# Linear attention and two MLPs on one core: decays loaded once, weights landing where their halves go, a third attention buffer, and an opening in another order

## The chip, the cores and the metric

The kernel runs on one core of one Trainium2 chip. The core has five engines with their own instruction streams: TensorE (PE, matmuls; PEld are its weight loads), VectorE (DVE), ScalarE (ACT), GpSimd (POOL) and SyncE (SP, which here issues nearly all DMAs). The metric is the device time of one execution in microseconds (us), as the median of several runs. A profile is one further execution with the hardware profiler on.

## The reference

```python
# q, k, v, alpha: (4 batches, 8 heads, 768 tokens, 48), alpha between 0.8 and 1.0
for t in range(S):
    state = alpha[:, :, t, :, None] * state + einsum('bhd,bhe->bhde', k[:, :, t], v[:, :, t])
    y[:, :, t] = einsum('bhd,bhde->bhe', q[:, :, t], state)
x = y as 3072 tokens x 384
h = x @ w_in            # 384 x 2048
x = (h * sigmoid(1.702 * h)) @ w_out
h = x @ w2_in           # the same sizes, other weights
out = (h - tanh(h)) @ w2_out
```

All is fp32. The weights reach the kernel as 64-bit floats.

## The kernel before, in words

The attention is cut into 24 chunks g of 128 tokens, six to a batch. The 8 heads lie in 4 pairs. For a chunk, DVE forms running products of the decay along the tokens with two scans, one forwards (`a_scan(g, 1)`) and one backwards (`a_scan(g, 0)`, whose row is loaded reversed as a second copy of the same decays), a reciprocal between them, and multiplies keys and queries by them (`a_scale`, L249 and L250; on POOL from chunk 8 on). These steps are called `prep(g, 0..3)`. Then PE forms the scores (L279, or L298 from chunk 8 on), which are masked (POOL L285, or DVE L301 from chunk 8 on), the masked scores times the values (L332), the carried state times the queries (L325), and the new part of the state (L341). ACT takes the result out of the bank (`a_evac`, L360), SP writes it to `xt` in device memory (L365) and reads it back turned (`a_back`, L378) as the MLP's input, of which ACT forms a high half (`xhi`, L382) and DVE the low rest (`xlo`, L383). From chunk 8 on DVE also turns the keys by 32x32 transposes (L308), because the whole chunk is then done in one go.

Each MLP layer goes over six tiles j of 512 tokens and 16 columns of blocks m: a step s is one pair (j, m), 96 steps to a layer. A step has nine 128x512 matmuls of gemm1 (L392: high x high, high x low, low x high over three blocks), the activation on ACT (L406 for layer 1), its split into `ghi` (ACT L409) and `glo` (DVE L410), and nine matmuls of gemm2 (L399), which PE does three steps later (LAG 3).

The weights of a layer arrive as 768 KB per m (L156) in one of three `raw` buffers. DVE rebuilds fp32 from the 64-bit form (`w_bits`, L163 and L164; `w_join`, L176), ACT copies the high half `whi` (L193) and DVE subtracts for `wlo` (L194). For layer 1 this happens during tile j=0, one m per step, in `conv(1)`; until then only three are ready. A raw buffer comes free when `w_join` of its m is done, and SP, which takes its orders strictly in turn, waits there.

Opening (chunks 0 to 3) and tile j=0 (with chunks 4 to 7 and the start of 8 and 9 beside it) are kept in the order of the program text by `in_order(begin)`. What comes after is ordered by a scheduler from the program text and its own priorities. From chunk 8 on every chunk's scans, transposes and masks run on DVE beside the MLP steps of layer 1 while PE takes the chunk's matmuls between its gemms. Attention chunk data lie in two late buffers of the `arena` (chunk 2 in `gt` and `xs`), and the load of chunk g+2 is issued when chunk g is done.

## Time and profile before

| | us |
|---|---|
| median of three runs | 952.52 |
| the three runs | 954.36, 948.78, 952.52 |
| the profiled execution | 957.78 |
| its span from first to last instruction | 956.1 |
| PE, DVE, ACT busy in it | 913.8 (96%), 676.5 (71%), 449.5 (47%) |
| DMA moved | 101.91 MB |

The profiled execution lies 5.3 us above the median. A row of a timeline gives start, duration, engine, line, operation, tiles, and in brackets the idle time of that engine before it and what ended it. Rows of PE that follow each other without a bracket ran without a gap. PEclk is the share of TensorE's full clock that was granted.

### The profile page before, as it was taken

The numbers are of one execution on the slowest core, as the hardware profiler recorded it, in microseconds if no ns is written. First come the engines' busy times: TensorE is split into PE (matmuls) and PEld (weight loads), VectorE is DVE, ScalarE is ACT, GpSimd is POOL, SyncE is SP. The second block draws the span as 40 slices with busy tenths as digits, with TensorE's granted clock in tenths as the row PEclk, the third lists the DMA queues.
The fourth block names the chain that finished last, engine by engine and source line by source line (L and its number), as shares of the span: only waits on it lengthen the run. The fifth ranks groups of instructions, "written<-read, shape, count | busy, mean of one in ns | idle before, by whom it ended". The sixth has DMA issues, their size and how long they took to land.

```text
span 956.1 us, 13257 instructions
## 1 busy us (share of the span) xinstructions
PE 913.8 (96%) x4870; PEld 728.1 (76%) x4870; DVE 676.5 (71%) x1124; ACT 449.5 (47%) x906; POOL 85.9 (9%) x70
## 2 busy tenths in 40 slices
PE   5569999999989999999999999999999999999997
PEld 4347777777768777777888888888888888888885
DVE  7799997844774787484159986766776777766663
ACT  4445533323434434343344564554566566544542
POOL 1201211101120111110100200100100001000000
PEclk9999999989989999999999999999999999999999
DMA  9767434422643565434125410200322420000001
GB/s 268 236 201 240 137 87 125 120 68 79 200 132 141 159 196 198 128 113 158 32 93 181 138 60 1 78 22 1 113 96 89 166 99 1 33 1 1 34 1 37
DMA packets 58107, 101.91 MB, mean 107 GB/s; under 512 B 5024, under 2 KB 37408, under 8 KB 58032
## 3 DMA queue, kind: packets, MB, share of 16 engines
q1 hardware_dynamic: 58032, 100.97, 33.7%
q8 instruction: 40, 0.66, 0.3%
q14 instruction: 35, 0.29, 0.1%
HBM read 86.79 MB, written 14.16 MB: 106 GB/s over the span
## 4 chain that ended last, share of the span: by engine, by line
PE 61%; DVE 0%; issue 0%; ACT 0%; ACTq 0%
PE bank L399 30%; PE bank L392 29%; PE bank L332 1%; PE bank L298 0%; PE bank L325 0%; PE bank L341 0%; DVE xs L442 0%; DVE arena L301 0%; PE bank L268 0%; ACT xs L445 0%; ACTq L671 0%
## 5 line engine op out<-in xcount | busy, mean ns | idle before, releaser
L410 DVE TENSOR_TENSOR glo<-gt,ghi 128x512 fp32r<-128x512 f32 x192 | 140.1, 732 | 151.0 <-ACT ghi L409 146.8
L392 PE MATMUL bank<-xhi,whi 128*128 128x512 f32 x576 | 229.2, 398 | 9.5 <-ACT xhi L382 8.8
L399 PE MATMUL bank<-ghi,whi 128*128 128x512 f32 x576 | 233.1, 405 | 0.0
L399 PE MATMUL bank<-ghi,wlo 128*128 128x512 f32 x576 | 229.0, 397 | 0.0
L392 PE MATMUL bank<-xlo,whi 128*128 128x512 f32 x576 | 228.5, 397 | 0.4 <-DVE xlo L383 0.4
L399 PE MATMUL bank<-glo,whi 128*128 128x512 f32 x576 | 228.5, 397 | 0.0
L392 PE MATMUL bank<-xhi,wlo 128*128 128x512 f32 x576 | 228.1, 396 | 0.0
L409 ACT CAST ghi<-gt 128x512 fp32r<-128x512 f32 x192 | 119.2, 621 | 220.8 <-DVE gt L421 133.1
L392 PEld LDWEIGHTS bank<-xhi,whi 128*128 128x128 f32 x576 | 109.2, 190 | 35.6 <-ACT xhi L382 9.0
L399 PEld LDWEIGHTS bank<-ghi,whi 128*128 128x128 f32 x576 | 109.2, 190 | 28.4 <-issue 1.9
L392 PEld LDWEIGHTS bank<-xlo,whi 128*128 128x128 f32 x576 | 109.3, 190 | 26.4 <-DVE xlo L383 1.2
L399 PEld LDWEIGHTS bank<-glo,whi 128*128 128x128 f32 x576 | 109.4, 190 | 25.7
L392 PEld LDWEIGHTS bank<-xhi,wlo 128*128 128x128 f32 x576 | 109.1, 189 | 25.5
L399 PEld LDWEIGHTS bank<-ghi,wlo 128*128 128x128 f32 x576 | 109.5, 190 | 24.2 <-issue 0.5
L406 ACT ACTIVATE gt<-bank 128x512 f32<-128x512 f32 x96 | 57.4, 597 | 95.6 <-PE bank L392 72.0
L308 DVE STREAM_TRANSPOSE cf<-arena 32x128 f32<-32x128 f32 x256 | 77.5, 303 | 24.9 <-PE bank L341 10.0
L419 DVE SCALAR_TENSOR_TENSOR arena<-arena,bank 128x512 f32<-128x512 f32 x96 | 65.8, 686 | 29.4 <-ACT arena L417 28.6
L421 DVE SCALAR_TENSOR_TENSOR gt<-arena 128x512 f32<-128x512 f32 x96 | 68.3, 712 | 10.9 <-DVE arena L420 1.4
L417 ACT ACTIVATE arena<-bank 128x512 f32<-128x512 f32 x96 | 57.3, 597 | 36.1 <-PE bank L392 35.7
L243 DVE TENSOR_TENSOR_SCAN arena<-arena,seg 112x516 f32<-112x516 f32 x46 | 63.5, 1380 | 14.6 <-DMA arena<-xq 13.6
L418 ACT ACTIVATE arena<-arena,cs 128x512 f32<-128x512 f32 x96 | 69.6, 725 | 2.9
L420 DVE SCALAR_TENSOR_TENSOR arena<-arena 128x512 f32<-128x512 f32 x96 | 67.9, 707 | 3.0
(89 smaller groups left out, 663.2 us busy)
## 6 DMA issues: line engine op xcount, KB each, us to landing
raw<-w SPq DMA_DIRECT2D x64, 768.0 KB, 4.5
arena<-xq SPq DMA_DIRECT2D x46, 224.0 KB, 4.4
arena<-xq SPq DMA_DIRECT2D x22, 451.5 KB, 5.1
xlo<-xt SPq DMA_DIRECT2D x24, 192.0 KB, 4.4
x1t<-xs SPq DMA_DIRECT2D x6, 768.0 KB, 3.4
arena<-x1t SPq DMA_DIRECT2D x6, 768.0 KB, 4.5
out<-xs SPq DMA_DIRECT2D x18, 256.0 KB, 2.3
arena<-xv SPq DMA_DIRECT2D x23, 192.0 KB, 3.3
```

The lines of the kernel that those rows point to most:

```text
L243: V.tensor_tensor_scan(out=dec(g, n), data0=src(g, n), data1=seg, initial=0.0, op0=ALU.mult, op1=ALU.max)
L308: V.transpose(out=d[32 * y : 32 * y + 32], in_=k[32 * x : 32 * x + 32, :, 32 * y : 32 * y + 32])
L392: P.matmul(out=h, lhsT=w[m][:, ws], rhs=x[:, k, :n], start=c == 0, stop=c == 3 * KT - 1)
L399: P.matmul(out=acc[k][:, :n], lhsT=w[m][:, ws], rhs=x[s % 3][:, :n], start=m == 0 and c == 0, stop=m == MT - 1 and c == 2)
L406: A.activation(out=gf[i][:, :n], in_=h, func=AF.Silu, scale=1.702)
L409: A.copy(ghi[s % 3][:, :n], gf[s % 2][:, :n])
L410: e.tensor_tensor(out=glo[s % 3][:, :n], in0=gf[s % 2][:, :n], in1=ghi[s % 3][:, :n].bitcast(F32), op=ALU.subtract)
L417: A.activation(out=u, in_=h, func=AF.Square, accum_out=usum[:, s - NS1 :][:, :1])
L418: A.activation(out=w, in_=u, func=AF.Square, bias=pbias)
L419: V.scalar_tensor_tensor(out=p, in0=u, scalar=P3, in1=h, op0=ALU.mult, op1=ALU.mult)
L420: V.scalar_tensor_tensor(out=p, in0=u, scalar=-PR, in1=p, op0=ALU.add, op1=ALU.mult)
L421: V.scalar_tensor_tensor(out=gf[i], in0=w, scalar=PD, in1=p, op0=ALU.add, op1=ALU.mult)
```

## The change

Five things are changed together.

- The decays of a chunk are loaded once. The backward scan reads the same row from its end (`[:, AW:0:-1]`), and what it writes is read reversed where it is used. Each row gets one more column, which small memsets fill.
- A layer-1 weight lands in a tile `given[m]` that has the place where `whi[m]` and `wlo[m]` will stand, so that no raw buffer is waited for. Loads go up to six m ahead. The 768 columns of `wlo` and `whi` are written once the 64-bit words have been read.
- The first two raw buffers hold a third attention chunk (`spare`, chunks 3, 6, 9, ...), and the load of chunk g+3 is issued when chunk g is done. Layer 2's weights still go through raw.
- The opening has another order: scores of a chunk one ahead of the chunk's output, 69 matmuls whose result nobody reads (`idle`, 128x512, written to bank 2), the input constants on ACT's queue, one activation that reads nothing of use and has the Silu function, in front.
- In tile j=0 the stages of chunks 4 to 7 start two steps later, and `conv(1)` is written behind the activation of the step instead of behind gemm1. The check of the weights (`w_check`, in tiles 2 and 3 of both layers) uses one raw buffer instead of three.

The core of the diff:

```diff
-    raw = [T(f"raw{i}", (128, WC, 2), I32) for i in range(3)]
+    given = [sb.tile([128, WC, 2], I32, name=f"given{m}", tag=f"w{m}") for m in range(MT)]
+    rawb = T("raw", (128, 3 * WC * 2), I32)
...
+    spare = chunk(rawf[:, :QW], rawf[:, QW : QW + VW])
...
+    def w_given(m):
+        SP.dma_start(out=given[m], in_=w1[m].bitcast(I32).rearrange("p (n t) -> p n t", t=2))
...
+    def w_hi(l, m):
+        if l == 1:
+            t = sb.tile([128, 2 * WC], F32R, name=f"w{m}", tag=f"w{m}")
+            whi[m], wlo[m] = t[:, :WC], t[:, WC:]
+        A.copy(whi[m], cfs[l][m % len(cfs[l])])
...
+    def place_of(g):
+        return third if g == 2 else (spare, *late)[g % 3] if g > 2 else late[g]
...
         if n == 0:
             V.memset(first, 1.0)
-        V.tensor_tensor_scan(out=dec(g, n), data0=src(g, n), data1=seg, initial=0.0, op0=ALU.mult, op1=ALU.max)
-        if n == 0:
+            V.tensor_tensor_scan(out=dec(g, 0), data0=src(g, 1)[:, AW:0:-1], data1=seg, initial=0.0, op0=ALU.mult, op1=ALU.max)
             V.reciprocal(out=first, in_=dec3(g, 0)[:, :, C:])
+        else:
+            V.tensor_tensor_scan(out=dec(g, 1), data0=dec(g, 1), data1=seg, initial=0.0, op0=ALU.mult, op1=ALU.max)
...
+    def idle(n):
+        w = seg[:, 1:65].bitcast(BF16)
+        for _ in range(n):
+            P.matmul(out=bank[2], lhsT=w, rhs=w.unsqueeze(1).to_broadcast([DP, 4, 128]), start=True, stop=True)
...
+    idle(18)
+    for r in range(2):
+        s_mm(0, r, (5, 3)[r])
...
+    idle(8)
     for g in range(4):
         if g < 3:
             for r in range(3):
                 prep(g + 1, r)
+            for r in range(2):
+                s_mm(g + 1, r, (5, 3)[r])
+        if g == 3:
+            w_bits(1, 0)
+            w_join(1, 0)
+        if g:
+            a_state(g - 1)
+        a_out(g, 0)
+        idle((3, 3, 3, 34)[g])
...
         a_evac(g, 0)
         a_guard(g)
+        a_back(g)
...
+    w_lo(1, 0)
+    w_bits(1, 1)
+    x_hi(0)
+    w_join(1, 1)
+    x_lo(0)
...
+    x_hi(3)
+    x_lo(3)
...
-            elif l == 1:
-                conv(1)
-                fetch()
...
             if l == 1 and j == 0:
                 sig_1(s, h, n)
+                q, r = divmod(m - 2, 3)
+                if r == 2 and 0 <= q < 4:
+                    a_done(q + 4)
+                    a_state(q + 4)
...
+                conv(1)
+                if m + 6 < MT:
+                    w_given(m + 6)
```

On SP, in the place after the opening, the loads of the weights and the writes of chunk 4's result to `xt` stood before as follows (`raw` are the three buffers, L365 the writes, the rest the load of chunk 6):

```order
L156 DMA raw_95<-w 128x1536
L156 DMA raw_96<-w 128x1536
L156 DMA raw_97<-w 128x1536
L156 DMA raw_95<-w 128x1536
L365 DMA xt<-arena 48x2x128 x4
L232 DMA arena<-xq 112x1032
L234 DMA arena<-xq 112x512
L236 DMA arena<-xq 112x4x128
L238 DMA arena<-xv 128x384
```

Now, up to the same writes (L390) and the load of the next chunk:

```order
L162 DMA given_68<-w 128x1536
L162 DMA given_69<-w 128x1536
L162 DMA given_70<-w 128x1536
L162 DMA given_71<-w 128x1536
L162 DMA given_72<-w 128x1536
L390 DMA xt<-arena 48x2x128 x4
L403 DMA xlo_88<-xt 128x3x128
L251 DMA arena<-xq 112x516
```

Five weights go in front of the writes instead of four, each to a place of its own, and the chunk's decays are 516 columns instead of 1032.

On DVE, at the end of tile j=0 (L383 is the low rest of chunk 7's input, which the first gemm of tile j=1 needs; L301 are chunk 8's masks; L308 transposes the keys of chunks 8 and 9), before:

```order
L383 TENSOR_TENSOR xlo_106<-xlo_106,xhi_104 128x3x128
L308 STREAM_TRANSPOSE cf_101<-arena 32x4x32 x2
L243 SCALAR_TENSOR_TENSOR arena<-arena,seg 112x516
L308 STREAM_TRANSPOSE cf_101<-arena 32x4x32
L410 TENSOR_TENSOR glo_112<-gt,ghi_109 128x512
L245 RECIPROCAL seg<-arena 112x4
L243 SCALAR_TENSOR_TENSOR arena<-arena,seg 112x516
L242 MEMSET seg 112x4
L410 TENSOR_TENSOR glo_113<-gt,ghi_110 128x512
L410 TENSOR_TENSOR glo_111<-gt,ghi_108 128x512
L301 TENSOR_TENSOR arena<-bank_128,cs 128x512
L301 TENSOR_TENSOR arena<-bank_129,cs 128x512
```

Now (L411 is chunk 7's low rest, L326 the masks, L333 the transposes):

```order
L258 SCALAR_TENSOR_TENSOR arena<-arena,seg 112x516
L333 STREAM_TRANSPOSE cf_82<-arena 32x4x32 x2
L333 STREAM_TRANSPOSE cf_83<-raw 32x4x32
L442 TENSOR_TENSOR glo_95<-gt,ghi_92 128x512
L333 STREAM_TRANSPOSE cf_83<-raw 32x4x32 x2
L259 RECIPROCAL seg<-arena 112x4
L411 TENSOR_TENSOR xlo_88<-xlo_88,xhi_86 128x3x128
L442 TENSOR_TENSOR glo_93<-gt,ghi_90 128x512
L261 SCALAR_TENSOR_TENSOR arena<-arena,seg 112x516
L326 TENSOR_TENSOR arena<-bank_110,cs 128x512
L326 TENSOR_TENSOR arena<-bank_111,cs 128x512
```

Chunk 7's low rest now stands behind all 32 transposes of the place, with four instructions between it and the last mask where there were ten (three transposes among them).

On DVE again, in front of the masks of chunk 11, before:

```order
L243 SCALAR_TENSOR_TENSOR arena<-arena,seg 112x516
L245 RECIPROCAL seg<-arena 112x4
L243 SCALAR_TENSOR_TENSOR arena<-arena,seg 112x516
L242 MEMSET seg 112x4
L243 SCALAR_TENSOR_TENSOR arena<-arena,seg 112x516
L301 TENSOR_TENSOR arena<-bank_128,cs 128x512
L301 TENSOR_TENSOR arena<-bank_129,cs 128x512
```

Now:

```order
L258 SCALAR_TENSOR_TENSOR arena<-arena,seg 112x516
L442 TENSOR_TENSOR glo_95<-gt,ghi_92 128x512
L259 RECIPROCAL seg<-arena 112x4
L261 SCALAR_TENSOR_TENSOR arena<-arena,seg 112x516
L257 MEMSET seg 112x4
L258 SCALAR_TENSOR_TENSOR raw<-raw,seg 112x516
L259 RECIPROCAL seg<-raw 112x4
L261 SCALAR_TENSOR_TENSOR raw<-raw,seg 112x516
L326 TENSOR_TENSOR arena<-bank_110,cs 128x512
L326 TENSOR_TENSOR arena<-bank_111,cs 128x512
```

Four scans, of two chunks, now stand right in front of these masks where three stood.

## Rows read from the trace of the kernel before

**Rows 1.** Timeline of PE (start, us, engine line op), opening and first steps.
```profile
8.20 3.03 PE L279 MATMUL bank<-arena 48*128 48x176 f32 x16 [8.20 <-DVE seg L242]
...
30.31 2.72 PE L279 MATMUL bank<-arena 48*128 48x176 f32 x16
47.41 0.80 PE L392 MATMUL bank<-xhi,whi 128*128 128x512 f32 x1 [8.79 <-ACT xhi L382]
...
55.77 0.87 PE L279 MATMUL bank<-arena 48*128 48x176 f32 x8
57.32 0.50 PE L392 MATMUL bank<-xhi,whi 128*128 128x512 f32 x1 [0.69 <-ACT gt L406]
...
63.30 0.40 PE L392 MATMUL bank<-xlo,whi 128*128 128x512 f32 x1
63.53 0.40 PE L392 MATMUL bank<-xhi,wlo 128*128 128x512 f32 x1
69.99 1.55 PE L279 MATMUL bank<-arena 48*128 48x176 f32 x8 [6.06 <-issue]
```

**Rows 2.** Windows: stretch, length, busy time of PE, PEld, DVE, ACT, POOL, PEclk, DMA.
```profile
191.90:198.80 6.90, 6.85 (x37) 5.30 (x38) 6.29 (x18) 1.36 (x3) 1.19 (x1) 0.51 0.39 101
...
277.20:284.10 6.90, 6.12 (x47) 4.90 (x48) 3.81 (x11) 0.74 (x2) 2.14 (x2) 0.51 0.24 61
284.10:949.00 664.90, 663.97 (x3202) 534.13 (x3201) 453.19 (x715) 329.56 (x643) 42.98 (x30) 1.00 0.26 85
```

**Rows 3.** Windows, the stretch from 49.00 to the end of chunk 8's masks.
```profile
49.00:144.04 95.04, 86.99 (x524) 66.59 (x523) 89.99 (x144) 47.02 (x102) 14.04 (x13) 0.96 0.55 163
```

**Rows 4.** Timeline of DVE, opening and first steps of j=0.
```profile
4.19 1.23 DVE L243 TENSOR_TENSOR_SCAN arena<-arena,seg 112x516 f32<-112x516 f32 x1 [0.79 <-DMA arena<-xq]
...
8.05 0.06 DVE L242 MEMSET seg<- 112x4 f32 x1
9.48 1.23 DVE L243 TENSOR_TENSOR_SCAN arena<-arena,seg 112x516 f32<-112x516 f32 x1 [1.37 <-DMA arena<-xq]
...
47.39 0.56 DVE L383 TENSOR_TENSOR xlo<-xlo,xhi 128x384 fp32r<-128x384 f32 x1 [2.77 <-ACT xhi L382]
...
65.67 0.95 DVE L176 SCALAR_TENSOR_TENSOR cf<-raw,cf 128x768 int32<-128x768 int32 x1
66.53 0.56 DVE L163 TENSOR_SCALAR cf<-raw 128x768 int32<-128x768 int32 x1
67.13 0.96 DVE L164 SCALAR_TENSOR_TENSOR cf<-raw,cf 128x768 int32<-128x768 int32 x1
...
69.21 0.68 DVE L250 TENSOR_TENSOR arena<-arena 112x512 f32<-112x512 f32 x1
69.81 0.35 DVE L352 TENSOR_TENSOR state<-bank,state 112x192 f32<-112x192 f32 x1
```

**Rows 5.** Timeline of SP, the wait for raw buffers.
```profile
49.98 17.00 SPq L156 DMA_DIRECT2D raw<-w  x4
```

**Rows 6.** Timeline of DVE, end of tile j=0.
```profile
120.73 0.95 DVE L194 TENSOR_TENSOR wlo<-cf,whi 128x768 fp32r<-128x768 f32 x1
...
136.53 0.56 DVE L383 TENSOR_TENSOR xlo<-xlo,xhi 128x384 fp32r<-128x384 f32 x1
...
142.76 1.28 DVE L301 TENSOR_TENSOR arena<-bank,cs 128x512 f32<-128x512 f32 x2
```

**Rows 7.** Timeline of PE, the two later stalls.
```profile
191.35 0.42 PE L325 MATMUL bank<-arena,state 48*48 48x128 f32 x4 [1.45 <-DVE arena L301]
...
277.98 1.69 PE L325 MATMUL bank<-arena,state 48*48 48x128 f32 x16 [3.04 <-DVE arena L301]
```

**Rows 8.** Timeline of DVE, scans ahead of these two stalls.
```profile
185.56 1.23 DVE L243 TENSOR_TENSOR_SCAN arena<-arena,seg 112x516 f32<-112x516 f32 x1 [0.88 <-DMA arena<-xq]
...
188.45 2.27 DVE L243 TENSOR_TENSOR_SCAN arena<-arena,seg 112x516 f32<-112x516 f32 x1
...
274.48 1.23 DVE L243 TENSOR_TENSOR_SCAN arena<-arena,seg 112x516 f32<-112x516 f32 x1 [1.52 <-DMA arena<-xq]
```

More of the change, by code (lines that the diff above doesn't have):

```diff
@@ L78, in T @@
         return sb.tile(list(shape), dt, name=name)
-    whi = [T(f"whi{m}", (128, WC), F32R) for m in range(MT)]
-    wlo = [T(f"wlo{m}", (128, WC), F32R) for m in range(MT)]
-    raw = [T(f"raw{i}", (128, WC, 2), I32) for i in range(3)]
+    whi, wlo = {}, {}
+    given = [sb.tile([128, WC, 2], I32, name=f"given{m}", tag=f"w{m}") for m in range(MT)]
+    rawb = T("raw", (128, 3 * WC * 2), I32)
+    raw = [rawb[:, 2 * WC * i : 2 * WC * (i + 1)].rearrange("p (n t) -> p n t", t=2) for i in range(3)]
     wtb = T("wtb", (128, WC))
@@ L252, in a_guard @@
     def a_guard(g):
-        t = (gt if g == 2 else lateb[(g + (g > 2)) % 2])[:DP, : 2 * AW]
+        t = (gt if g == 2 else rawf if place_of(g) is spare else arena[:, (QW + VW) * late.index(place_of(g)) :])[:DP, : 2 * AW]
         A.activation(out=t, in_=t, func=AF.Square, accum_out=guard[:, g : g + 1])
@@ L279, in a_scores, with s_copy @@
                 P.matmul(out=o[hh][:, i], lhsT=k[r, 2 * x + i], rhs=q[r, 2 * x + i], start=True, stop=True)
+    def s_copy(g, x, b, turned):
+        u = (2 * g + x) % 2
+        o = [bank[b + hh][:, : 2 * CE].rearrange("p (a t) -> p a t", a=2) for hh in range(2)]
         s4 = sm[u].rearrange("p (b a t) -> p b a t", b=2, a=2)
         kt = kts[u].rearrange("p (b a t) -> p b a t", b=2, a=2)
+        if turned:
+            for hh in range(2):
+                A.copy(kt[:, hh], o[hh][:, :, C:])
+            return
         for hh in range(2):
@@ L286, in a_scores @@
                         compare_op=ALU.is_ge, fill=0.0)
-        for hh in range(2):
-            A.copy(kt[:, hh], o[hh][:, :, C:])
+    def a_scores(g, x, b):
+        s_mm(g, x, b)
+        s_copy(g, x, b, False)
+        s_copy(g, x, b, True)
     def a_whole(g, b):
@@ L303, in a_turn @@
     def a_turn(g, low):
-        k = pairs(late[(g + (g > 2)) % 2][3])
+        k = pairs(place_of(g)[3])
         for x in (0, 2) if low else (1, 3):
@@ L529, in in_order @@
             last[ins.engine] = ins.name
+    def idle(n):
+        w = seg[:, 1:65].bitcast(BF16)
+        for _ in range(n):
+            P.matmul(out=bank[2], lhsT=w, rhs=w.unsqueeze(1).to_broadcast([DP, 4, 128]), start=True, stop=True)
     begin = len(nc.cur_bb.bb.instructions)
     V.memset(seg, A_MIN)
-    a_load(0, (0, 1, 2, 3))
-    SP.dma_start(out=cs, in_=cst)
-    a_load(1, (0, 1))
-    a_load(0, (4,))
-    for _, t in enumerate(late):
-        SP.dma_start(out=t[3][DP:], in_=xq[0, : 128 - DP, : NP * C])
-    a_load(1, (2, 3, 4))
-    a_load(2)
-    w_load(1, 0)
-    w_load(1, 1)
+    for t in (*late, third, spare):
+        V.memset(t[1][:DP, AW:], 0.0)
+    A.dma_start(out=cs, in_=cst)
+    A.activation(out=fine[:1, :1], in_=seg[:1, 1:2], func=AF.Silu)
+    a_load(0, (1, 3, 2))
+    for g in (1, 2, 3):
+        a_load(g, (1,))
+        a_load(g - 1, (4,))
+        a_load(g, (3, 2))
+    a_load(3, (4,))
+    w_given(0)
     for b in (0, 1, 7):
@@ L628, in linear_attention_mlps @@
                 sig_1(s, h, n)
-                if m % 3 == 2 and m < 12:
-                    a_done(m // 3 + 4)
-                    a_state(m // 3 + 4)
-                if m % 3 == 0 and 0 < m < 13:
-                    prep(m // 3 + 4, 3)
-                if m % 3 == 1 and m > 3:
-                    a_x(m // 3 + 3)
+                q, r = divmod(m - 2, 3)
+                if r == 2 and 0 <= q < 4:
+                    a_done(q + 4)
+                    a_state(q + 4)
+                if r == 0 and 0 < q < 5:
+                    prep(q + 4, 3)
+                if r == 1 and q > 0:
+                    a_x(q + 3)
+                conv(1)
+                if m + 6 < MT:
+                    w_given(m + 6)
+                if m == 6:
+                    for t in (*late, spare):
+                        SP.dma_start(out=t[3][DP:], in_=xq[0, : 128 - DP, : NP * C])
             if 2 <= j < 4 and m % 2:
```

150 lines of the change are left out of this document (79 added, 71 removed).

## The prediction

> **What bounds the kernel now.** I read the busy shares first, then the timeline of PE from the opening on for its gaps, then for each gap the timeline of the engine that ended it, and last the windows for TensorE's granted clock. The whole is PE's: from 284 to 949 us its matmuls fill 663.97 of 664.90 us [rows 2], and nothing in the change takes a matmul out of those. What can change is what comes before: the first gemm, which begins at 47.41 after PE had waited 8.79 for the high half of chunk 3's input [rows 1], and the stalls after it. There are three.
>
> The first is the largest: 6.06 us before the chunk-5 scores at 69.99. The profile names no releaser, but the last instruction that they need, the scaling of the queries on DVE, starts at 69.21 [rows 1, 4]. SP stands still for 17.00 us at the raw buffers in the same stretch [rows 5]; that is a symptom, because the buffers come free when DVE has joined a weight. The window from 49.00 to 144.04 shows why: DVE is busy 89.99 of 95.04 us, more than PE with 86.99 [rows 3]. So tile j=0 is bound by DVE, not by PE. The other two are at 191.35 and 277.98: PE waits 1.45 and 3.04 us for the masks of a chunk [rows 7], and each is followed by 6.9 us at a granted clock of 0.51, which is the level of 1.2 GHz instead of 2.4 [rows 2]. In front of those masks DVE does scans, and the first of them had waited for the load of its decays, 0.88 and 1.52 us [rows 8].
>
> The sum is made in the profiled execution, 957.78 us with a span of 956.1. That lies 5.3 us above the median of 952.52; I take what is saved off both.
>
> **The change part by part: the opening.** DVE gets its first decays at 4.19, and a prep takes from 4.19 to 8.05, 3.86 us [rows 4]; both stay, since a backward scan has the same number of elements. Four preps are 15.4 us, so they end at 19.6 at the earliest. Before, the second had to wait 1.37 for a load of both decay rows [rows 4]; now half the bytes are asked for, but a fourth chunk's too, so I add 2.5 for waits and slow rows: 22.1. The first weight's three conversions are 0.56 + 0.96 + 0.95 = 2.5, and five state instructions of 0.35 are 1.8 [rows 4]: 26.4. Then DVE waits for the high half of the first weight, which stands on ACT behind the copies of chunks 0 to 3. No row shows that wait; between none (26.4) and 33, I take 30. From there to chunk 3's low rest the new order has three low halves (0.95 [rows 6]), two more conversions (2.5), four low rests (0.56) and one scan (1.23): 2.9 + 5.0 + 2.2 + 1.2 = 11.3, so 41.3, and the first gemm starts at about 42.0 instead of 47.4. Each result's way over `xt` and back lies beside this, as far as the chunks before chunk 3 go.
>
> Against it stands PE itself. Sixteen chunk-3 score matmuls took 2.72 us in the opening, while eight took 0.87 at full clock later: the opening's attention ran at the half clock [rows 1]. The 69 added matmuls are there in PE's queue ahead of and between the chunks. If they raise the clock, PE's own chain ends in time for 42. If it falls back between chunks, a chunk takes PE some 8 us as before (the fourth scores at 30.31 come 22.1 us after the first at 8.20, some 7.4 each [rows 1]), and the 34 last ones still stand before the gemm; PE then reaches it at about 50. The Trainium skill, "TensorE: Matmul & The Clock Gate" (section "What's actually happening"), has it that the throttled state is the default and that activity releases it. By that rule the start would be 42 and the sum below would stand as it is; by the row of the attention matmuls, which stayed at half clock here [rows 1], it would be 50, and the median 949. No row shows the added matmuls, so the trace bears the rule out only from the first gemms on (eight scores in 0.87 at 55.77 [rows 1]).
>
> The bounds of the start are 38 and 50, the value 42.
>
> **Tile j=0.** DVE's work here does not shrink: the same conversions, glo's, transposes and scans in another order. From the first gemm at 47.41 to the masks' end at 144.04 it is 96.6 us [rows 1, 6]. After the change one low half (0.95) has gone in front of the gemm; chunk 4's second scan (1.2), a state update (0.7) and chunk 9's scan with its reciprocal (1.4) stand behind it, +3.3; and DVE's idle of 95.04 - 89.99 = 5.05 [rows 3] shrinks by some 3.4 by my estimate, since no conversion waits for a load any more. So 96.6 - 0.95 + 3.3 - 3.4 = 95.6, and with 1.0 for the tighter lead (ACT's copy of a weight now stands behind the activation of its step) 96.6 again: the masks end at 138.6, 5.4 us earlier. Not all of that is PE's. Chunk 7's low rest, at 136.53 before, was 7.5 us in front of the masks' end [rows 6]; now it stands behind all transposes, with a glo, a scan and the masks after it, 0.56 + 0.7 + 1.2 + 1.3 = 3.8 before their end, at 134.8. PE's own work up to there is some 84 us by an estimate (the 87.0 of the window [rows 3], 1.6 before it, less about 5 behind the first gemm of tile 1), so PE is there at 126 and waits up to 8.8 us, longer than the wait at 69.99 which this one replaces. A gemm2 is still owed at this place, 9 x 0.23 = 2.1 us at the spacing of full clock [rows 1], so 3.3 are left; and behind the wait at 69.99 the clock was at half (1.55 for eight score matmuls against 0.87 [rows 1]), which costs the nine gemm1 matmuls 2.1 more. Gain of the first phase: 1.2 to 3.3; I take 2. With the start at 38 it would be up to 6, with 50 about -2 (DVE can go on some 6 us ahead of PE before it needs gemm results, so a late PE costs less than its delay).
>
> **The later stalls.** They cost 1.45 + 3.4 and 3.04 + 3.4 us (half of 6.9 at the half clock is lost): 11.3 in all [rows 2, 7]. The third buffer lets a chunk's load be issued one chunk earlier, so the waits of 0.88 and 1.52 go [rows 8]. What is late next is the DVE queue itself. The first stall shrinks to 0.57; a gap of 0.69 at 57.32 left the clock as it was [rows 1], so the half-clock stretch goes too: 0.88 + 3.4 = 4.3. The second shrinks to 1.52, and a stall of 1.45 lost the clock [rows 7], so there only 1.5 is won. Together 5.8; bounds 0 (DVE does an additional pair of scans in front of the masks, as the order of chunk 11 shows) and 11.3.
>
> **At nothing.** 24 decay rows less, some 5.4 MB of 101.9: the later part of the run has DMA to spare, as the windows show (0.24 to 0.39 of the engines' time) [rows 2]. Strided reads of the decays: rows of L250 and of the strided conversions cost by elements (0.68 for 512, 0.96 for 768) [rows 4]. The load of the Silu function moves in front. The four memsets and the 16-row loads lie beside DMA waits; if that cover is gone they cost under 1 us.
>
> Sum: 957.78 - 2 - 5.8 = 950.0 for an execution like the profiled one, and 952.52 - 7.8 = 944.7 as a median. I predict 945.
>
> **The rivals.**
> - All of it works: DVE has its lead, PE's wait at chunk 7's low rest is short, and both later stalls go. Then 3.3 to 5.4 and 11.3 are won, 952.5 - 15.5 = 937. For it: the loads no longer wait for any raw buffer. Against it: DVE's 90 us of work in 95 [rows 3].
> - The stalls are the order's, not the loads': the scans stand a chunk further ahead, take the time that the waits took, and PE waits as before. Then only 1.2 is won: 951.
> - The opening stays at half clock and the gemm starts at 50: +2 there, -5.8 later: 949. For it: the 2.72 us of the scores at 30.31 [rows 1]. Against it: once the first gemms had run, the clock was up (0.87 for eight scores at 55.77 [rows 1]).
> - Slower: the scheduler puts more scans before the masks of chunks 9 to 23. The first stall's masks stood behind a scan that took 2.27 us instead of 1.23 [rows 8]; two scans more are 2.5 us and more, over the 1.45 that lost the clock. If two more chunks stall so, at 1.5 to 3 us and 3.4 each, that is 11.3 more instead of 5.8 less: 952.5 - 2 + 11.3 = 962. It decides when PE has more than two gaps of over 1.4 us before L350 between 145 and 400.
>
> **How the numbers follow.** A difference of 0.5%, 4.8 us, is about what a measurement of this kernel tells from none. The forecast (940 to 948) gets 0.40, all of it 0.15, the two cases that give 949 and 951 together 0.28, slower 0.17. Faster by over 0.5% (under 947.8) is the first two, less a little of the first's upper end, and comes to 0.53; within 0.5% 0.30; slower 0.17. The range leaves the far end of the slower case and the best of the good one out: 934 to 958; the forecast's own is 940 to 948.
>
> **What would show it.** The first gemm at 42 (right), at 47 or more (the opening's step wrong). In the opening, 16 score matmuls in 1.7 us instead of 2.7 (clock up). A wait of PE for chunk 7's low rest at the start of tile j=1, of 5 to 8 us, with the masks' end at 138 to 139. No wait of DVE for decay loads at the stalls near 190 and 275, one half-clock stretch there instead of two. The prediction is wrong if PE has a wait for weights in most steps of j=0, or if SP or ACT, not DVE, ends the long gaps.

## The result, and the profile after: 965.27 us, slower

The median went from 952.28 (four runs of the kernel before beside it) to 965.27 us: a ratio of 1.014, with an interval of 1.0108 to 1.0172. The forecast was 945, the range 934 to 958; the time is above both. The profiled execution took 965.55 us, span 963.5, so 7.8 more than the profiled one before; the other 5 us of the median's 13 are those by which the profiled execution before lay above its own median. The page's head and its row of the granted clock:

```profile
span 963.5 us, 13407 instructions
...
PE 929.2 (96%) x4939; PEld 728.8 (76%) x4939; DVE 672.9 (70%) x1128; ACT 449.4 (47%) x908; POOL 87.5 (9%) x70
...
PEclk9899989979999999999999999999999999999999
```

PE is busy 15.4 us longer than before (929.2 against 913.8), which says little, since the 69 matmuls added to the opening alone are 19.3. The row of the clock shows at which slices it fell short; of the first microseconds it does not tell, since the window from 8 to 47 us of the trace before reads 1.00, while 16 score matmuls took 2.72 there. Where the time goes is seen by the starts of gemm1 in the two traces, step by step (a step is one pair of j and m; the difference is after less before):

| step | 0 | 4 | 16 | 17 | 25 | 26 | 96 | 184 |
|---|---|---|---|---|---|---|---|---|
| before, us | 47.41 | 75.47 | 136.35 | 142.49 | 186.72 | 197.15 | 540.34 | 908.43 |
| difference | -0.25 | -11.9 | -1.6 | +2.6 | +3.6 | +8.1 | +6.0 | +7.5 |

Four places: the first gemm is not earlier; tile j=0 gives an interim lead back; at step 26 some 4.5 us are lost at once, of which the stretch up to step 96 gives about 2.6 back; and from step 96 to 184, where nothing waits, 1.5 more go. These 4.5 understate the loss: the trace before lost some 4.4 at this place itself, by a stall that two other traces with its order do not have (e5 and e7, shown with e6). Against those two, the new kernel loses some 9 there. The rows of PE in the new trace that answer to [rows 1] and [rows 7] (columns as there):

```profile
13.62 1.47 PE L294 MATMUL bank<-arena 48*128 48x176 f32 x16 [1.47 <-issue]
...
19.33 2.99 PE L294 MATMUL bank<-xs 48*128 48x176 f32 x16 [2.11 <-ACT xs L243]
...
28.54 2.01 PE L294 MATMUL bank<-raw 48*128 48x176 f32 x16 [1.42 <-ACT raw L243]
...
47.16 0.49 PE L424 MATMUL bank<-xhi,w 128*128 128x512 f32 x1 [1.28 <-ACT xhi L407]
49.70 0.51 PE L424 MATMUL bank<-xlo,w 128*128 128x512 f32 x1 [2.04 <-DVE xlo L411]
...
128.17 0.73 PE L424 MATMUL bank<-xhi,w 128*128 128x512 f32 x2 [2.38 <-DVE w L208]
...
142.31 0.50 PE L424 MATMUL bank<-xlo,w 128*128 128x512 f32 x1 [2.21 <-DVE xlo L411]
...
200.29 1.70 PE L350 MATMUL bank<-arena,state 48*48 48x128 f32 x16 [6.24 <-DVE arena L326]
...
285.24 0.42 PE L350 MATMUL bank<-raw,state 48*48 48x128 f32 x2 [1.74 <-DVE arena L326]
```

In the opening, chunk 1's scores take 1.47 us, chunk 2's 2.99 and chunk 3's 2.01: PE had the full clock and lost it, each time near a wait for L243, which is ACT's copy of an identity for that chunk's scores (the granted clock of the two stretches, 0.50, is in the windows below). The 6.06 us stall of before has become smaller ones. The carried state of chunk 11, at 191.35 before after a wait of 1.45, now waits 6.24. DVE's rows around those waits:

```profile
26.12 0.36 DVE L377 TENSOR_TENSOR state<-bank,state 112x192 f32<-112x192 f32 x1 [3.96 <-PE bank L366]
...
34.34 0.36 DVE L377 TENSOR_TENSOR state<-bank,state 112x192 f32<-112x192 f32 x1 [5.02 <-PE bank L366]
...
143.91 1.26 DVE L326 TENSOR_TENSOR arena<-bank,cs 128x512 f32<-128x512 f32 x2
...
173.40 1.28 DVE L326 TENSOR_TENSOR arena<-bank,cs 128x512 f32<-128x512 f32 x2
...
179.60 5.32 DVE L333 STREAM_TRANSPOSE cf<-arena 32x128 f32<-32x128 f32 x16 [1.08 <-POOL arena L265]
...
192.83 1.24 DVE L258 TENSOR_TENSOR_SCAN arena<-arena,seg 112x516 f32<-112x516 f32 x1 [0.74 <-DMA arena<-xq]
...
194.78 2.00 DVE L261 TENSOR_TENSOR_SCAN arena<-arena,seg 112x516 f32<-112x516 f32 x1
...
196.94 1.23 DVE L258 TENSOR_TENSOR_SCAN raw<-raw,seg 112x516 f32<-112x516 f32 x1
...
198.43 1.23 DVE L261 TENSOR_TENSOR_SCAN raw<-raw,seg 112x516 f32<-112x516 f32 x1
199.57 1.26 DVE L326 TENSOR_TENSOR arena<-bank,cs 128x512 f32<-128x512 f32 x2
```

In the opening DVE, which should have run ahead with weights, waits 3.96 and 5.02 us for PE. From the masks of chunk 10 (173.40) to those of chunk 11 (199.57) it takes 26.2 us, where the trace before has 20.6 (170.06 to 190.64). Between them stand 32 transposes instead of 16, the additional set being the row at 179.60 with its 5.32 us, and six scans instead of five; the last one before is the row at 188.45 of [rows 8]. The load of the decays is still waited for, 0.74 against 0.88. The windows (busy time of PE, PEld, DVE, ACT and POOL, with instructions; then granted clock, DMA share, GB/s) answer to [rows 2, 3]:

```profile
19.80:26.60 6.80, 6.80 (x65) 5.25 (x65) 2.81 (x5) 2.28 (x9) 1.27 (x2) 0.50 0.77 223
30.10:36.90 6.80, 6.80 (x65) 4.48 (x66) 0.72 (x2) 4.33 (x13) 1.27 (x2) 0.50 0.45 151
...
49.70:145.17 95.47, 87.31 (x523) 66.45 (x524) 93.33 (x147) 44.19 (x99) 17.11 (x14) 0.95 0.53 172
...
197.30:207.60 10.30, 7.30 (x41) 5.44 (x42) 5.04 (x8) 1.36 (x3) 1.18 (x1) 0.50 0.18 48
```

Tile j=0 is DVE's, 93.33 of 95.47 us. The stall at step 26 is followed by a half-clock stretch of some 10 us where 6.9 stood before.

### The profile page after: what moved, and what is told of

It reads as the page before. It is cut to its first block, busy times and chain, and to the rows that moved or that the text cites. A ratio compares the mean times of both kernels' runs of the same rounds, so it can differ in the third digit from the quotient of the medians.

```text
span 963.5 us, 13407 instructions
## 1 busy us (share of the span) xinstructions
PE 929.2 (96%) x4939; PEld 728.8 (76%) x4939; DVE 672.9 (70%) x1128; ACT 449.4 (47%) x908; POOL 87.5 (9%) x70
## 4 chain that ended last, share of the span: by engine, by line
PE 68%; DVE 2%; POOL 0%; issue 0%; ACT 0%; ACTq 0%
PE bank L431 33%; PE bank L424 32%; DVE cf L333 1%; PE bank L357 1%; PE bank L323 1%; PE bank L350 1%; PE bank L366 0%; POOL arena L265 0%; DVE xs L474 0%; DVE arena L326 0%; DVE wtb L179 0%; DVE glo L442 0%; ACT ghi L441 0%; DVE xlo L411 0%; DVE state L377 0%
## 5 line engine op out<-in xcount | busy, mean ns | idle before, releaser
L424 PE MATMUL bank<-xhi,w 128*128 128x512 f32 x1152 | 395.3, 398 | 3.7 <-DVE w L208 2.4
L431 PE MATMUL bank<-ghi,w 128*128 128x512 f32 x1152 | 368.4, 400 | 0.3 <-DVE xs L474 0.3
L424 PEld LDWEIGHTS bank<-xhi,w 128*128 128x128 f32 x1152 | 218.6, 190 | 57.5 <-DVE w L208 3.1
L431 PEld LDWEIGHTS bank<-ghi,w 128*128 128x128 f32 x1152 | 213.9, 189 | 54.0 <-issue 2.5
L424 PE MATMUL bank<-xlo,w 128*128 128x512 f32 x576 | 230.1, 400 | 4.2 <-DVE xlo L411 4.2
L431 PE MATMUL bank<-glo,w 128*128 128x512 f32 x576 | 228.2, 397 | 0.0
L424 PEld LDWEIGHTS bank<-xlo,w 128*128 128x128 f32 x576 | 109.4, 190 | 31.3 <-DVE xlo L411 4.7
L431 PEld LDWEIGHTS bank<-glo,w 128*128 128x128 f32 x576 | 108.5, 188 | 26.7
L453 DVE SCALAR_TENSOR_TENSOR gt<-arena 128x512 f32<-128x512 f32 x96 | 68.4, 712 | 10.5 <-DVE arena L452 0.9
L333 DVE STREAM_TRANSPOSE cf<-arena 32x128 f32<-32x128 f32 x176 | 53.3, 303 | 17.3 <-PE bank L366 7.2
L490 POOL TENSOR_TENSOR xlo<-arena,xhi 128x512 fp32r<-128x512 f32 x18 | 27.6, 1561 | 378.5 <-ACT xhi L489 378.5
L181 ACT ACTIVATE wtb<-wtb 128x768 bf16<-128x768 int16 x32 | 26.7, 835 | 17.1 <-DVE wtb L179 13.6
L270 ACT ACTIVATE arena<-arena 112x1032 f32<-112x1032 f32 x16 | 17.1, 1070 | 25.5 <-DVE state L378 19.3
L333 DVE STREAM_TRANSPOSE cf<-raw 32x128 f32<-32x128 f32 x80 | 24.2, 303 | 4.6 <-issue 1.4
```

Of the source, the lines that this page charges most:

```text
L333: V.transpose(out=d[32 * y : 32 * y + 32], in_=k[32 * x : 32 * x + 32, :, 32 * y : 32 * y + 32])
L424: P.matmul(out=h, lhsT=w[m][:, ws], rhs=x[:, k, :n], start=c == 0, stop=c == 3 * KT - 1)
L431: P.matmul(out=acc[k][:, :n], lhsT=w[m][:, ws], rhs=x[s % 3][:, :n], start=m == 0 and c == 0, stop=m == MT - 1 and c == 2)
L453: V.scalar_tensor_tensor(out=gf[i], in0=w, scalar=PD, in1=p, op0=ALU.add, op1=ALU.mult)
L490: G.tensor_tensor(out=xlo[i][:, k], in0=xr[:, k], in1=xhi[i][:, k].bitcast(F32), op=ALU.subtract)
```

## The experiments

Two theories were held from the start: A, the loss sits in the opening (ACT's identity copies cost PE its clock and DVE its lead) and in the third attention buffer (it lets the scheduler put more of DVE's work before a chunk's masks); B, the loss is in something that all of the new kernel has, such as the places of the weights. Ratios are to the kernel before on the same chip, with 95% intervals; differences between two variants are those of their medians. Most runs change one thing, of after, of before or of e4; e4 and e9 join two.

**e1_eyes: after, all four identity copies at the start.**

```diff
-    eye(0)
-    eye(1)
+    for g in range(4):
+        eye(g)
...
-            eye(g + 2)
```

> The changed kernel with the four identity copies (eye) of chunks 0 to 3 all written at the start on ACT, instead of those of chunks 2 and 3 behind the evacuations of chunks 0 and 1. Theory A (the score matmuls of chunks 2 and 3 wait 2.11 and 1.42 us for these copies, the clock falls to half at 19.8 and 30.1, and with it the first gemm comes at 47.2 and its second matmul at 49.7): the two waits go, the clock stays up, the first gemm's second matmul comes at 41 to 44, chunk 8's masks end 5 to 7 us earlier than 145.2, and the time falls by 4 to 8 us against the changed kernel. Rival B (the opening is bound elsewhere: the 34 idle matmuls, the way over device memory, or the weight loads): the waits go, the first gemm stays at 46 or later, and the time moves by less than 2 us.

Measured: 960.73, ratio 1.0087 (1.0056 to 1.0117), 4.5 us less than after. Its PE:

```profile
18.68 1.46 PE L294 MATMUL bank<-xs 48*128 48x176 f32 x16
...
22.93 1.47 PE L294 MATMUL bank<-raw 48*128 48x176 f32 x16
...
41.65 0.79 PE L424 MATMUL bank<-xhi,w 128*128 128x512 f32 x1 [4.54 <-ACT xhi L407]
42.24 0.79 PE L424 MATMUL bank<-xlo,w 128*128 128x512 f32 x1
```

The scores stay at 1.46 and 1.47, nothing waits for the low rest, and the first gemm starts at 41.65: 5.5 us earlier by the first matmul, 7.5 by the second. The rule of the Trainium skill, "TensorE: Matmul & The Clock Gate" (section "What's actually happening"), that activity releases the throttle, agrees with these rows and with e3, where the same scores take 3.08 and 3.09 without the added matmuls.

Of the 5.5 us of the opening 2.7 are left at step 17 (142.41 against 145.12): the masks of chunk 8 end 100.5 us behind the first gemm (in after 98.0), at 142.13, which is 3.0 earlier than in after and not the expected 5 to 7. The wait before chunk 11's carried state stays (6.27, in after 6.24).

**e2_two: after, two attention buffers as before, load of g+2.**

```diff
-        return third if g == 2 else (spare, *late)[g % 3] if g > 2 else late[g]
+        return third if g == 2 else spare if g == 3 else late[g % 2]
...
-        if g + 3 < NG:
-            a_load(g + 3)
+        if g + 2 < NG:
+            a_load(g + 2)
...
-    a_load(6)
```

> The changed kernel with two buffers for chunks 4 and up, as before (chunk 3 alone keeps its place in raw; the load of chunk g+2 is issued when chunk g is done). Theory A (the third buffer lets the scheduler put scans and transposes of later chunks in front of masks and of chunk 7's low rest): DVE's order at these places is that of the kernel before, PE's wait of 6.24 us before chunk 11's carried matmuls falls to 1.5 to 2, its half-clock stretch from 10.2 to 6.9 us or less, PE's waits around the start of tile 1 fall, and the time falls by 5 to 9 us. Rival B (the third buffer's saved load waits are worth more than the order costs): the time rises by 1 to 4 us, since the waits for decay loads come back.

Measured: 958.77, ratio 1.0056 (1.003 to 1.0083), 6.5 us less than after. DVE before chunk 11's masks, and PE behind them:

```profile
190.78 2.15 DVE L258 TENSOR_TENSOR_SCAN arena<-arena,seg 112x516 f32<-112x516 f32 x1
192.85 0.66 DVE L326 TENSOR_TENSOR arena<-bank,cs 128x512 f32<-128x512 f32 x1
```

```profile
193.57 0.42 PE L350 MATMUL bank<-arena,state 48*48 48x128 f32 x4 [0.31 <-DVE arena L326]
```

Between the masks of chunks 10 and 11 there are 16 transposes and four scans again (175.11 to 192.85, 17.7 us), and 6.24 us of wait have become 0.31, though DVE now waits longer for the load (1.52 at 187.44). So the buffer that was to end a wait for a transfer made the wait for DVE. Not all that is won at chunk 11 is kept: two new stalls, at 341.84 (1.59) and 360.03 (2.29), take about 5 us back between steps 48 and 64.

**e3_noidle: after without the 69 idle matmuls.**

```diff
-        for _ in range(n):
+        for _ in range(0):
```

> The changed kernel without the 69 idle matmuls, all else in place. Theory A (they hold the clock up for only part of the opening, 6.2 to 19.8 and 26.7 to 30.1 us, and cost PE nothing at the end): the opening's attention runs wholly at half clock, the first gemm comes 2 to 5 us later or at the same time, and gemms start at half clock, 2 us lost; the time rises by 1 to 5 us. Rival B (PE's queue of 34 of them before the first gemm is in the way): the first gemm starts earlier and the time falls by up to 2 us.

Measured: 968.74, ratio 1.0158 (1.0127 to 1.0189), 3.5 us more than after.

```profile
21.32 3.08 PE L294 MATMUL bank<-xs 48*128 48x176 f32 x16 [2.48 <-ACT xs L243]
...
50.09 0.79 PE L424 MATMUL bank<-xhi,w 128*128 128x512 f32 x1 [9.88 <-ACT xhi L407]
```

The two intervals overlap, so the times alone do not settle it; the rows do for the opening. Without the idle matmuls 16 scores take 2.72 to 3.09 us in all four chunks, twice the 1.47 at full clock, and the first gemm is 2.9 later.

**e4_eyes_two: e1 and e2 together** (both diffs above).

> Both edits together: identity copies at the start, and two buffers from chunk 4 on. If both theories A hold and the places are apart, the gains add: 9 to 15 us under the changed kernel, 950 to 956 as a median, near or just under the kernel before. If the first phase is bound by DVE alone, the earlier start is kept (masks of chunk 8 end at 137 to 140). If it is over 960, one of the two theories is wrong.

Measured: 955.23, ratio 1.0028 (1.0008 to 1.0048). The two gains add up: 10.0 less than after, where e1 and e2 gave 4.5 and 6.5. Some 3 us to the kernel before were left, and the masks of chunk 8 end at 142.49, not at 137 to 140. Two new rows caught the eye, on PE and on SP's queue:

```profile
137.45 0.80 PE L424 MATMUL bank<-xlo,w 128*128 128x512 f32 x1 [5.75 <-DVE xlo L411]
...
355.15 0.42 PE L350 MATMUL bank<-arena,state 48*48 48x128 f32 x2 [1.88 <-DVE arena L326]
```

```profile
38.34 0.37 SPq L165 DMA_DIRECT2D raw<-w  x1
39.64 0.40 SPq L403 DMA_DIRECT2D xlo<-xt  x1
```

A weight that only the check wants, tiles later, is loaded in the opening, ahead of chunk 3's way back; e2 has it too, at 41.75; after and e1, with three attention buffers, do not.

**e5_turns: before, whi and wlo allotted in turns.** A test of theory B: the places of the halves as in after.

```diff
-    whi = [T(f"whi{m}", (128, WC), F32R) for m in range(MT)]
-    wlo = [T(f"wlo{m}", (128, WC), F32R) for m in range(MT)]
+    whi, wlo = [], []
+    for m in range(MT):
+        whi.append(T(f"whi{m}", (128, WC), F32R))
+        wlo.append(T(f"wlo{m}", (128, WC), F32R))
```

> The kernel before with one thing changed: the tiles of the high and low weight halves are allotted in turns (whi0, wlo0, whi1, wlo1, ...), as the changed kernel's joint tiles place them, instead of all high halves ahead of all low ones. It bears on a small loss seen beside the stalls: steps 96 to 184, which have no stall in any trace, take 368.09 us in the kernel before and 369.60 in the changed kernel and in all four experiments on it. Theory A (the place of the halves costs PE about 1 ns a matmul): these 88 steps take 369.6, and the time rises by about 3 us. Rival B (it is from another source: the longer arena, the other start): they take 368.1 and the time does not move.

Measured: 953.25, ratio 1.0015 (0.9999 to 1.0031). The places are not the cause.

**e6_decays: before, with the decays loaded once and nothing else.**

```diff
-        V.tensor_tensor_scan(out=dec(g, n), data0=src(g, n), data1=seg, initial=0.0, op0=ALU.mult, op1=ALU.max)
...
+            V.tensor_tensor_scan(out=dec(g, 0), data0=src(g, 1)[:, AW:0:-1], data1=seg, initial=0.0, op0=ALU.mult, op1=ALU.max)
```

> The kernel before with the decays loaded once and the backward row read from its end, and nothing else of the change. Theory A (the decay loads' bytes are hidden but for the waits of 0.88 and 1.52 us in front of the two later stalls): the waits shrink by up to half a us each, the time moves by less than 2 us. Rival B (this part carries the gain that was forecast): DVE's waits for decay loads (13.6 us before) fall by half or more, the stalls at 190 and 275 us lose their half-clock stretches, and the time falls by 3 to 6 us.

Measured: 946.9, ratio 0.9938 (0.9919 to 0.9957), 5.4 us faster than before. DVE's waits for decay loads go from 13.6 to 5.9 us in all. The scan that reads its row from the end takes what a scan took, 1.23:

```profile
183.92 1.23 DVE L239 TENSOR_TENSOR_SCAN arena<-arena,seg 112x516 f32<-112x516 f32 x1 [0.55 <-DMA arena<-xq]
```

Where chunk 11 waited 1.45 in the trace before, PE has no wait. That is not the decays' doing: e5, which loads them twice, has next to none either (0.17), though its DVE waited longer for the load (1.25 against 0.88); in e7 it is 0.27, with 1.49 for the load. DVE, POOL and PE of e5:

```profile
184.54 1.23 DVE L245 TENSOR_TENSOR_SCAN arena<-arena,seg 112x516 f32<-112x516 f32 x1 [1.25 <-DMA arena<-xq]
...
187.42 1.23 DVE L245 TENSOR_TENSOR_SCAN arena<-arena,seg 112x516 f32<-112x516 f32 x1
```

```profile
187.65 1.98 POOL L251 TENSOR_TENSOR arena<-arena 112x512 f32<-112x512 f32 x1 [10.64 <-DMA arena<-xq]
```

```profile
189.89 0.64 PE L327 MATMUL bank<-arena,state 48*48 48x128 f32 x12 [0.17 <-DVE arena L303]
```

What the trace before has instead is the row at 188.45 of [rows 8], 2.27 for a scan of 1.23. POOL had begun 0.02 us ahead of it:

```profile
188.43 1.20 POOL L249 TENSOR_TENSOR arena<-arena 112x512 f32<-112x512 f32 x1 [10.50 <-DVE seg L242]
```

In e5 DVE began first, the scan took 1.23 and POOL's instruction 1.98. So the first of the two stalls hung on which engine came first in one execution. With its half-clock stretch it makes up most of the 5.3 us by which that execution lay above its median; whether other executions of the kernel before have it was not profiled. The decays show at the next stall, 1.30 against 3.69 in e5 (3.51 in e7):

```profile
271.01 0.42 PE L322 MATMUL bank<-arena,state 48*48 48x128 f32 x2 [1.30 <-DVE arena L298]
```

```profile
273.48 1.70 PE L327 MATMUL bank<-arena,state 48*48 48x128 f32 x16 [3.69 <-DVE arena L303]
```

By the spans the trace of e6 is 3.5 us shorter than that of e5 and 1.9 shorter than that of e7; the rest of the 5.4 is not placed. So the change holds a part that is worth nearly the gain that was forecast from the later stalls.

**e7_given: before, with layer-1 weights landing where their halves go, and nothing else.**

```diff
+    def raw_of(layer, m):
+        return given[m] if layer == 1 else raw[m % 3]
...
-        r, f = raw[m % 3], cfs[l][m % len(cfs[l])]
+        r, f = raw_of(l, m), cfs[l][m % len(cfs[l])]
```

> The kernel before with layer 1's weights landing in the tiles of their halves, loads issued in the same places as before, and nothing else of the change. Theory A (SP's wait of 17 us for raw buffers is a symptom of DVE's backlog): SP no longer waits, but PE's first stall near 64 us stays at 4 to 6 us, chunk 8's masks end within 1.5 us of 144.0, and the time does not fall by more than 1 us, or rises by up to 3 with the place of the halves. Rival B (the raw buffers bound tile j=0): the first stall goes and the time falls by 3 to 8 us.

Measured: 951.38, ratio 0.9988 (0.9968 to 1.0008): no difference. SP's 17.00 of [rows 5] are gone and the stall of PE is there all the same, 1.0 us shorter:

```profile
44.92 5.02 SPq L159 DMA_DIRECT2D given<-w  x4
```

```profile
69.67 1.35 PE L288 MATMUL bank<-arena 48*128 48x176 f32 x8 [5.06 <-issue]
```

**e8_pool: e4, with four low halves on GpSimd** in place of DVE, which bounds tile j=0.

```diff
-        V.tensor_tensor(out=wlo[m], in0=f, in1=whi[m].bitcast(F32), op=ALU.subtract)
+        e = G if l == 1 and m in (4, 7, 10, 13) else V
+        e.tensor_tensor(out=wlo[m], in0=f, in1=whi[m].bitcast(F32), op=ALU.subtract)
```

> The two edits together (identity copies at the start, two buffers from chunk 4 on) and besides the low halves of the weights 4, 7, 10 and 13 formed on GpSimd instead of VectorE. Theory A (tile j=0 is bound by DVE's sum of work): DVE has 4 x 0.95 = 3.8 us less to do, chunk 8's masks end 2 to 4 us earlier than 142.5, PE's wait of 5.75 us for chunk 7's low rest shrinks by as much, and the time falls by 2 to 4 us against the two edits. Rival B (GpSimd slows DVE beside it, as in the rows of 1.94 and 2.22 us, or a weight comes late): no gain, or up to 4 us slower, with PE waiting for these four halves.

Measured: 959.19, ratio 1.0072 (1.005 to 1.0095), 4 us more than e4. The expectation of a gain failed: one takes GpSimd 1.83 to 2.79 us, where DVE takes 0.95. In front of chunk 5's scores PE waits 2.05 (0.88 in e4) and the clock falls, and the masks of chunk 8 end at 145.71 instead of 142.49. DVE did not gain, either, as rival B had it: beside each of the four an instruction of its own became longer (at 58.47 one of 0.69 took 2.33; at 77.83, 95.55 and 112.84 ones of 0.95 took 2.32, 2.51 and 2.31). That is 5.9 us more on DVE, against the 3.8 taken off it. The Trainium skill, "GPSIMD Engine Reference" (section "4.1 Engine selection"), puts two-input elementwise work there at about twice DVE's time; these rows agree at the low end and go to 2.9 times.

```profile
111.54 2.79 POOL L209 TENSOR_TENSOR w<-xs,w 128x768 fp32r<-128x768 f32 x1 [1.53 <-ACT w L204]
```

```profile
112.84 2.31 DVE L185 SCALAR_TENSOR_TENSOR xs<-given,xs 128x768 int32<-128x768 int32 x1
```

**e9_both: before, with e6 and e7 together** (both edits, with the fitting tile places).

> The kernel before with two parts of the change, the decays loaded once and layer 1's weights landing where their halves go, the opening, the order of tile j=0 and the two buffers being as before. Theory A (the decays part is worth 5.4 us through the load waits of the late stalls, the weights part about 1 us in the first): the gains add, 945 to 947 as a median, 0.5 to 0.75% under the kernel before, and steps 96 to 184 take 368.1 us. Rival B (the parts overlap, or the landing collides with the decay loads): 948 or more. If the 88 steps take 369.6, the places of the tiles that only these two parts make together slow PE.

Measured: 946.44, ratio 0.9937 (0.9915 to 0.9958), as e6 alone. Steps 96 to 184 take 368.09 us as before, with weights and chunks placed as in after; so neither these places nor these two parts make PE's steady work slower.

**e10_one: e4, with one more matmul in the opening.** A test of whether the number of matmuls ahead, odd or even, sets the steady spacing.

```diff
+    P.matmul(out=bank[2][:, :176], lhsT=seg[:48, 0:128], rhs=seg[:48, 0:176], start=True, stop=True)
```

> The kernel with identity copies at the start and two buffers, and one more small fp32 matmul (48 rows, 176 columns) in the opening whose result nobody reads. It bears on the 1.5 us that steps 96 to 184 take longer in the changed kernel and all its variants, where matmul spacings alternate between 229.4 and 237.2 ns while the kernel before has an even 232.4. Theory A (the place of PE's instructions in their stream, odd or even, makes it): one instruction more turns it back, the 88 steps take 368.1 us, and the time falls by about 3 us to 952. Rival B (where the tiles lie, or anything else): the spacing stays alternating, 369.6, and the time stays at 955.

Measured: 961.45, ratio 1.0073 (1.005 to 1.0096). The steady spacing is unchanged (steps 96 to 184 in 369.6). But the trace counts the one matmul as two (4941 on PE against 4939), so an even number was added, and this run does not test odd against even. e3 does: it has 69 fewer, and 369.6 all the same. So that idea fell, by e3.

The run is flawed for its time, too. The matmul reads a tile that DVE writes again; DVE waited 3.99 us for it, and PE then 4.18 for the queries and keys of chunk 1. The scores behind that took 2.72 instead of 1.47, the first gemm came at 49.05 instead of 43.75, and the whole took 6.2 more. How much of this is the clock, and how much DVE's own delay, was not separated.

**e11_checks: e4, the weight check through three raw buffers as before.**

```diff
-        tc.keep_in_program_order(V.tensor_scalar(out=t, in0=w_high(raw[2]), scalar1=0x3800, scalar2=0x7800,
+        tc.keep_in_program_order(V.tensor_scalar(out=t, in0=w_high(raw[m % 3]), scalar1=0x3800, scalar2=0x7800,
...
-                tc.keep_in_program_order(w_load(l, 8 * (j - 2) + m // 2, 2))
+                tc.keep_in_program_order(w_load(l, 8 * (j - 2) + m // 2))
```

> The kernel with identity copies at the start and two buffers, and the check of the weights in tiles 2 and 3 going through three raw buffers in turn, as before, instead of one. Theory A (the one buffer makes SP hold back the decay load behind it, which ends in the half-clock stretch at 357 us): that stretch and the wait of 1.88 us before it go, and the time falls by 3 to 4 us to 951 or 952. Rival B (the load lands late for another reason): no change, 955.

Measured: 944.7, ratio 0.9912 (0.9889 to 0.9935), 10.5 us less than e4; 3 to 4 had been expected. No check weight is loaded in the opening any more, the first gemm is 2.0 earlier, and the stall near 355 is gone:

```profile
41.76 0.79 PE L424 MATMUL bank<-xhi,w 128*128 128x512 f32 x1 [4.80 <-ACT xhi L407]
...
133.82 0.80 PE L424 MATMUL bank<-xlo,w 128*128 128x512 f32 x1 [5.74 <-DVE xlo L411]
...
349.41 0.66 PE L350 MATMUL bank<-arena,state 48*48 48x128 f32 x16
```

By rows, 3.6 us of the gain are in place by step 17 (133.82 against 137.45). The stalls of e4 at 337.38 and 355.15 were 1.04 and 1.88 with 3.4 us at the half clock behind; e11 has one of 1.86 at 268.09 instead, with none. Between steps 48 and 64, where those two stood, 5.7 are won, and some 1.5 are lost at the stall of 268.09. That makes up the 8.0 by which the profiled executions differ; the rest of the 10.5 is that e4's lies 1.3 under its median and e11's 1.3 above.

**e12_sp: e11, with the constants back on SP's queue and without the early Silu.**

```diff
-    A.dma_start(out=cs, in_=cst)
-    A.activation(out=fine[:1, :1], in_=seg[:1, 1:2], func=AF.Silu)
...
+    SP.dma_start(out=cs, in_=cst)
```

> The kernel with identity copies at the start, two buffers and three raw buffers for the checks (944.7), with two more lines of the opening put back: the constants are loaded on SP's queue behind chunk 0 instead of on ACT's queue, and the Silu activation that reads nothing of use is left out. It bears on the 1.5 us that steps 96 to 184 take longer in the changed kernel and its variants, which neither the places of the weight halves, nor the tiles, nor one more matmul explained. Theory A (a queue or a function table left from the opening makes it): the 88 steps take 368.1 us, and the time falls by 2 to 3 us to 942. Rival B (neither): they take 369.6, the function table is loaded before the first Silu of the steps (1.3 us) and the constants come later, so the time stays or rises by up to 2 us, 944.7 to 947.

Measured: 943.9, ratio 0.9907 (0.9882 to 0.9933), the lowest median of all and faster than both kernels; against e11 no difference that can be told.

```profile
40.70 0.49 PE L424 MATMUL bank<-xhi,w 128*128 128x512 f32 x1 [4.42 <-ACT xhi L407]
```

Its masks of chunk 8 end at 137.9, and behind 133 no wait of PE is over 0.5 us.

## Why the prediction was wrong, by its own steps

**The opening (42.0 instead of 47.4): wrong, by a missing term.** The step counted DVE's preps and conversions, and of ACT the high half of the weight. It did not look at where ACT's identity copies of chunks 2 and 3 had gone: behind the copies out of the bank and the guard of the chunk before. The wait that was to end at 30, DVE's for the high half of the first weight, ended at 37.22 in after, and at 29.41 in e1. ACT's rows of after:

```profile
26.40 0.66 ACT L385 COPY wtb<-bank 112x256 f32<-112x256 f32 x2
27.08 1.06 ACT L270 ACTIVATE arena<-arena 112x1032 f32<-112x1032 f32 x1
...
28.14 0.72 ACT L243 COPY raw<-cs 48x192 f32<-48x192 f32 x2
```

The copies for chunk 3, 0.72 in all, wait for their turn until 28.14, PE waits 1.42 for them, the clock stays at half, and DVE idles some 9 us. e1 moves the copies and nothing else, and the first gemm starts at 41.65. So the price with the clock up, 42, was right, in part by luck: in e1 the last wait is for chunk 3's way over `xt` (its high half starts at 41.09, when the load has landed), and DVE's chain, which the step added up, happens to end with it. The price of 50 without is near after's 47.16 and 49.70 and e3's 50.09. What chose between them were copies that the step had not looked for. The rival of 949 had this opening, but with the gain of 5.8 behind it.

**Tile j=0 (masks 96.6 behind the first gemm, DVE-bound): right for after, too short for the start that it was meant for.** In after the masks end 98.0 behind the first gemm, 95.5 behind 49.70, where the gemms go on. The step's remark that a start at 50 would cost about 2 fits the 2.6 at step 17. But in e1, which starts at 41.65, it is 100.5, and step 17 comes 0.1 earlier than in the trace before, not 2; with two attention buffers and three raw ones (e11) it is 97.1 and 5.5 earlier. The wait for chunk 7's low rest, put at up to 8.8 for a start at 42, is 5.74 in e11, and 2.21 in after and in e1. It goes with the buffers, not with the start: e2, which starts at 47.95, has 5.72. With three buffers other waits of over 2 us stand ahead of it (2.38 and 2.05 in after).

**The later stalls (5.8 won, bounds 0 and 11.3): wrong in sign, out of its bounds.** From step 17 to 96 after lost 3.4 us instead. Two things in the step failed. The first stall, priced at 4.3, was put down to the load of the decays; e5 and e7 wait longer for that load and do not have the stall, which came from a scan of 2.27 beside POOL in an execution 5.3 above the median. So the 4.3 was likely not there, or not wholly, to be won off the median. And the step gave the third buffer a gain. The decays without it (e6) win 5.4, near the 5.8, by other terms. The buffer's own effect is e2's: 6.5 us lost. A chunk's 16 transposes (5.32) and one scan (1.23) stand on DVE ahead of the masks that PE wants; that they do so because their data are there earlier is the reading of the orders with two buffers and with three. The lower bound of 0 had been set for "an additional pair of scans in front of the masks"; it thought of the scans, which the load feeds first, and not of the transposes that follow from them, and held that they would cost only what the waits had cost.

**The slower rival (962)** had the mechanism, more work before the masks, though it named scans and the larger part was transposes. It wanted more than two gaps of over 1.4 us before L350 between 145 and 400; there were two, of which one had grown to 6.24. So by its own condition it did not decide; the time near its 962 comes from another sum.

**At nothing:** the landing weights, right (e7). The single buffer of the check was in the list of changes and got no price; with two attention buffers it costs 10.5 us (e4 to e11). What it costs within after itself, where the third chunk needs the space, was not run. e11, the change without these three losses, takes 944.7, the very number of the forecast; that is luck, since it is added up from other terms.

**Left open.** Steps 96 to 184 take 368.09 us in before, e5, e6, e7 and e9 and 369.6 in every kernel with the new opening (after, e4, e10 to e12 among them), about 3 us over the whole. The same stretch in after, then in before:

```profile
540.00:900.00 360.00, 360.00 (x1544) 289.57 (x1544) 262.69 (x374) 200.64 (x403) 23.76 (x15) 1.00 0.17 58
```

```profile
540.00:900.00 360.00, 360.00 (x1551) 291.86 (x1550) 261.54 (x375) 200.47 (x404) 21.97 (x14) 1.00 0.17 58
```

Both are at full clock without a gap, with seven matmuls fewer in 360 us. Excluded are the weights' places (e5, e7), tile addresses and decays (e9), the idle matmuls and with them odd against even (e3), two matmul records more (e10), and the queue of the constants with the Silu (e12). The order of the opening and of tile j=0 is what remains; it was not taken back by itself.

## What to carry to other kernels

When work is moved earlier, list for every engine what it now stands behind, small copies too: copies of 0.72 us on an engine that seemed idle set the clock of another. A buffer more is no free gain where a scheduler orders the queues: a load that lands earlier may put its consumers ahead of work that the bounding engine waits for. Before a stall is priced, look for it in a second trace: one of the two here was there in one trace of three, and a row that took 2.27 instead of 1.23 was the sign of it. Take such a change apart: here one part was worth 5.4 us, one nothing, and three took back more (the place of the copies 4.5, the third buffer 6.5, the check's single buffer 10.5 beside two attention buffers).
